# Adding a block's FFN rows to h in memory, and transforming the first filter block directly

## The chip, the cores and the metric

The kernel runs on one core of a Trainium2 chip. The metric is device time in microseconds of one execution, the median of the runs shown. The engines are TensorE (PE, with its weight loads PEld), VectorE (DVE), ScalarE (ACT), GpSimd (POOL) and SyncE (SP), which here only issues transfers.

## The reference

```python
k_shift = sum over t of k_pad[:, t:t + S, :] * shift_k[:, ks - 1 - t]   # ks = 4 taps
kv = k_shift * v
y  = irfft(rfft(kv, 2S) * rfft(ssm_k, 2S))[:S] + kv * ssm_D             # long causal convolution
h  = x + layernorm(x) * y                                               # x = q
h2 = h + (silu(layernorm(h) @ w_gate) * (layernorm(h) @ w_up)) @ w_down
```

S is 2048, D is 640, the FFN width is 1728, all in bf16. `h2` is the output.

## The kernel before

The sequence is cut into four blocks of 512 rows, each held as 128 partitions x 4 rows (`r`) x 640. For each block j the kernel makes a spectrum of kv and one of the filter block g, multiplies and accumulates the spectra of the earlier blocks with those of the filter, transforms back, forms h, and runs the FFN on it. FFN j-1 is written to run beside the convolution part of block j.

A spectrum is four real parts times two halves, held in a buffer `S` of 128 x 2 x 4 x 640. `transform` first makes the sums over the even rows (r = 0, 2) and the odd rows (r = 1, 3) by two products each (`sums_of`, L298), copies both out of PSUM (L303, by ACT or DVE), and then DVE makes odd minus and plus even (L318, L321). In block 0 this is done in two column halves of 320 (`SPLIT`). `mac` multiplies spectra on DVE (L442 for the first term, L464 and L465 for the others); `inverse` makes the back transform (DVE L529, L532, then products L540), normalises x (`applied`, L516), multiplies with the product in PSUM (L547) and adds to x (L550), so that x's buffer then holds h. `square_sums` (L475), `ln1` (L509) and `norm` give the two LayerNorms' statistics; ln1's `norm` runs on POOL. `turn_h` normalises h and transposes it to hT (L564, L566).

`ffn` makes gate and up products (L591) in seven weight groups, loaded by SP into two buffers `wgu`; ACT makes silu (L597) and copies the up part (L606), DVE multiplies them (L608) into tT. Then for each of four rows r it makes the down products (L641), two halves of 14 each, into one PSUM buffer. Ahead of the first of them stand two products of h with the identity (L637), which add h. ACT copies the row to `o` (L645), and SP stores it (L646). There is one `o` buffer, two PSUM buffers `ps_c` for the convolution and two `ps_f` for the FFN. Two buffers `x` hold q and then h; the next block's q can be loaded only when h is no longer read.

No operation is issued directly: each is added to a `Plan` with a duration, a priority, its buffers and dependences, and `schedule` picks again and again the operation that can start first by its estimates (`key = (at, prio, number)`). The result is a fixed order on each engine. An operation with an `other` way is placed on whichever of two engines can take it first. At run time each engine works through its list in order and waits for semaphores. So a change of one duration in the plan can move instructions on every engine.

Before the first block the queue of SP holds, in order, tapw and ident (small), k, v, the transform table WF, g, one row D, x, the back table WI and the first weights. DVE builds the diagonal tap matrices `diag` (L660) from ident and tapw; TensorE transposes k (L415) and convolves with `diag` (L429), and DVE multiplies by v (L432).

## Time and profile before

| | |
|---|---|
| runs | 309.61, 308.06, 307.67 us; median 308.06 |
| profiled execution | 308.97 us, its span 306.7 us |
| busy | PE 92%, DVE 75%, ACT 55%, POOL 11% of the span |
| mean granted TensorE clock | 0.967 |
| moved by DMA | 34.41 MB, mean 112 GB/s |

A busy TensorE is not TensorE at its peak, since products are pipelined and their ends modelled: in a row of a group, the mean duration of one product is its latency, and its pace is read from the chain, where the time of several is given. In a row of the chain stand the start, the time and the group with its count.

### The profile page before, as it was taken

The page shows a single profiled execution, that of the slowest core. Times are in us where ns is not written, and L with a number is a line of the kernel's source. Part 1 is how long each engine was busy: PE and PEld are TensorE (multiplying, and loading weights), DVE is VectorE, ACT ScalarE, POOL GpSimd, SP SyncE. Part 2 cuts the span into 40 slices and gives each one's busy share as a digit, 9 for nine tenths or more (in the row PEclk, how much of TensorE's full clock was granted, in tenths as well). Part 3 has the DMA queues.
Part 4 walks back from the last instruction along what each step waited for, and adds up shares of the span by engine and source line. Part 5 has one row for each costly group of instructions (what it writes and reads, how often), then busy time and mean ns, then how long its engine had stood idle before and what let it go on. Part 6 is the DMA issues. An engine that isn't in the chain of part 4 may idle for free.

```text
span 306.7 us, 4908 instructions
## 1 busy us (share of the span) xinstructions
PE 283.2 (92%) x1964; PEld 173.3 (56%) x1964; DVE 231.1 (75%) x316; ACT 168.6 (55%) x285; POOL 34.7 (11%) x52
## 2 busy tenths in 40 slices
PE   1994777799999999999999999999998999999995
PEld 1962445675555657665455578654444665444563
DVE  3599987988999999999979899999989840110200
ACT  2198967727875444548866770368743532445301
POOL 0000800810000000000270000001490000000000
PEclk9999795599999999999999999999999999999999
DMA  6999300114736250343651330316564001654011
GB/s 214 371 344 355 92 1 12 76 37 134 205 96 187 51 130 21 110 128 94 167 128 21 97 98 24 92 41 164 138 146 129 23 24 52 164 146 89 2 43 43
DMA packets 51512, 34.41 MB, mean 112 GB/s; under 512 B 12641, under 2 KB 49698, under 8 KB 51490
## 3 DMA queue, kind: packets, MB, share of 16 engines
q1 hardware_dynamic: 51490, 34.11, 38.5%
q8 instruction: 15, 0.25, 0.3%
q14 instruction: 7, 0.06, 0.1%
HBM read 31.48 MB, written 2.62 MB: 111 GB/s over the span
## 4 chain that ended last, share of the span: by engine, by line
PE 78%; DVE 12%; ACT 4%; POOL 2%; DMA 1%; issue 1%; SPq 0%; DVEq 0%; ACTq 0%; POOLq 0%
PE ps_f L591 32%; PE ps_f L641 20%; PE ps_c L298 8%; PE ps_c L429 6%; PE ps_c L540 4%; DVE S L442 2%; PE ps_f L637 2%; DMA ld<-in_A_k_dram 1%; PE ps_c L564 1%; ACT sg L606 1%; PE ps_c L415 1%; DVE row L547 1%; DVE S L321 1%; DVE S L318 1%; PE ps_f L429 1%
## 5 line engine op out<-in xcount | busy, mean ns | idle before, releaser
L591 PE MATMUL ps_f<-hT,wgu 128*128 128x512 bf16 x540 | 122.1, 379 | 0.0
L591 PEld LDWEIGHTS <-wgu 128*128 128x128 bf16 x540 | 52.3, 98 | 57.5 <-issue 0.3
L641 PE MATMUL ps_f<-wd,tT 128*128 128x320 bf16 x448 | 67.4, 299 | 0.0
L641 PEld LDWEIGHTS <-tT 128*128 128x128 bf16 x448 | 42.1, 98 | 19.4 <-issue 4.0
L597 ACT ACTIVATE sg<-ps_f 128x1024 bf16<-128x1024 f32 (+1 forms) x28 | 27.0, 963 | 31.5 <-PE ps_f L591 31.5
L608 DVE TENSOR_TENSOR tT<-sg,sg 128x1024 bf16<-128x1024 bf16 (+1 forms) x28 | 18.2, 650 | 33.1 <-ACT sg L606 32.9
L298 PE MATMUL ps_c<-t,WF 128*128 128x320 bf16 x224 | 39.8, 312 | 2.0 <-ACT scr L303 0.8
L465 DVE TENSOR_TENSOR S<-S,scr 128x2560 bf16<-128x2560 bf16 x24 | 35.8, 1492 | 0.8
L298 PEld LDWEIGHTS <-WF 128*128 128x128 bf16 x256 | 25.4, 101 | 18.5 <-issue 5.2
L464 DVE TENSOR_TENSOR scr<-S,S 128x2560 bf16<-128x2560 bf16 x24 | 35.6, 1484 | 0.0
L606 ACT CAST sg<-ps_f 128x1024 bf16<-128x1024 f32 (+1 forms) x28 | 26.6, 949 | 16.5 <-PE ps_f L591 15.2
L645 ACT CAST o<-ps_f 128x640 bf16<-128x640 f32 x16 | 11.1, 692 | 42.6 <-PE ps_f L641 41.6
L475 ACT ACTIVATE row<-x 128x640 bf16<-128x640 bf16 x32 | 23.5, 739 | 14.2 <-DVE x L550 13.7
L429 PEld LDWEIGHTS <-kT 128*128 128x128 bf16 x320 | 21.3, 107 | 1.8 <-DVE kT L417 0.7
L303 ACT CAST scr<-ps_c 128x640 bf16<-128x640 f32 (+1 forms) x30 | 19.2, 672 | 5.4 <-PE ps_c L298 5.2
L490 POOL TENSOR_TENSOR sm<-sm 128x4 f32<-128x4 f32 x4 | 3.1, 763 | 160.2 <-ACT row L509 160.2
L429 PE MATMUL ps_c<-diag,kT 128*128 128x128 bf16 x280 | 19.0, 231 | 0.2 <-ACT hT L566 0.2
L303 ACT CAST S<-ps_c 128x640 bf16<-128x640 f32 (+1 forms) x25 | 15.3, 643 | 4.9 <-PE ps_c L298 4.9
L540 PEld LDWEIGHTS <-WI 128*128 128x128 bf16 x128 | 12.6, 98 | 9.4 <-issue 3.8
L516 DVE TENSOR_SCALAR row<-x,sm 128x640 bf16<-128x640 bf16 x32 | 12.9, 442 | 1.4 <-POOL sm L502 1.2
L432 DVE TENSOR_TENSOR t<-ps_c,ld 128x640 bf16<-128x640 f32 x14 | 11.2, 819 | 2.4 <-PE ps_c L429 2.4
L547 DVE SCALAR_TENSOR_TENSOR row<-row,ps_c 128x640 bf16<-128x640 bf16 x14 | 11.5, 820 | 1.6 <-PE ps_c L540 0.5
(80 smaller groups left out, 291.2 us busy)
## 6 DMA issues: line engine op xcount, KB each, us to landing
wgu<-in_B_w_gate_dram SPq DMA_DIRECT2D x24, 320.0 KB, 3.1
wgu<-in_B_w_up_dram SPq DMA_DIRECT2D x24, 320.0 KB, 3.2
ld<-in_A_k_dram SPq DMA_DIRECT2D x4, 640.0 KB, 4.5
ld<-in_A_v_dram SPq DMA_DIRECT2D x4, 640.0 KB, 5.0
ld<-in_A_ssm_k_dram SPq DMA_DIRECT2D x4, 640.0 KB, 5.4
x<-in_A_q_dram SPq DMA_DIRECT2D x4, 640.0 KB, 6.0
out_dram<-o SPq DMA_DIRECT2D x16, 160.0 KB, 1.8
wd<-in_B_w_down_dram SPq DMA_DIRECT2D x1, 2080.0 KB, 12.0
```

Source lines behind the costliest of these rows:

```text
L298: nc.tensor.matmul(ap(ps)[:, w, 0:NH], ap(WF)[:, r, c, :], ap(src)[:, r, w * NH:(w + 1) * NH], start=(i == 0), stop=(i == 1))
L303: copy(two(cut(to(c)[2](), ws)) if len(ws) == 2 else cut(to(c)[2](), ws), half(ap(ps)) if len(ws) == 2 else ap(ps)[:, ws[0], 0:NH])
L429: nc.tensor.matmul(line(ap(ps))[:, c * P:(c + 1) * P], ap(kT)[:, c, q, off:off + P], ap(diag)[:, 4 * c + t, :], start=(t == 0), stop=(t == 3))
L464: nc.vector.tensor_mul(flat2(b), X.part(xs), H.part(hs))
L465: f(A.part(dst), A.part(dst), flat2(b))
L475: act(930, lambda r=r, junk=junk: nc.scalar.activation(ap(junk), ap(x)[:, r, :], ACT.Square, scale=D ** -0.5, accum_out=sm(s, 1)[:, r:r + ...
L540: nc.tensor.matmul(ap(ps)[:, w, 0:NH], ap(WI)[:, c, r, :], src[:, w * NH:(w + 1) * NH], start=(c == 0), stop=(c == 3))
L591: nc.tensor.matmul(ap(ps)[:, i, :], ap(w)[:, k, off:off + P], ap(hT)[:, k, :], start=(k == 0), stop=(k == KT - 1))
L597: act(580 * n + 20 if n == 1 else 1010, lambda: nc.scalar.activation(ap(sg)[:, 0:n, :], ap(gate[0])[:, gate[1]:gate[1] + n, :], ACT.Silu), ...
L606: nc.scalar.copy(ap(co)[:, 0:n, :], ap(up[0])[:, up[1]:up[1] + n, :])
L608: op.rest = dve(420 if n == 1 else 690, lambda: nc.vector.tensor_mul(ap(tT)[:, c:c + n, :], ap(sg)[:, 0:n, :], ap(co)[:, 0:n, :]), [sg, co ...
L641: nc.tensor.matmul(ap(ps)[:, hf, 0:NH], ap(tT)[:n, c, r * P:(r + 1) * P], ap(wd)[:n, c, hf * NH:(hf + 1) * NH], start=False, stop=(c == NC ...
```

## The change

Five things change together.

- In blocks 0 to 2 the identity products are gone. SP stores h of the whole block to the output (L634 in the new kernel) once h is complete; ACT copies the FFN row to `o` as before (L694), and a transfer issued by POOL adds it to the output in memory (L698). In block 3 DVE adds h while it reads the row from PSUM (L692), and SP stores it.
- The first g spectrum is made `straight`: each of its two halves by four products per part, with a table `minus` of negated weights for the odd rows, so that no add or subtract follows. The products per part are four in place of two. `minus` lies in the FFN's `tT` buffer, which is free then, and is one more load of 128 x 2048.
- The first loads: tapw and ident are issued by ACT; x comes right behind k, ahead of v; minus behind g.
- LN1 of block 0 has its `norm` on DVE in place of POOL. In blocks 2 and 3 kv's PSUM rows may be copied by ACT and multiplied on DVE from SBUF (`ACTKV`), and rows may be normalised by ACT (`ACTLN`), with the bias that `norm` now makes; `inverse` may place its row normalisations ahead of the products.
- The plan's estimates: a POOL transfer holds POOL's queue for 1300 ns and ends 1600 ns behind its data, POOL's norm takes 10000 for 4000, `applied` 450 for 260; down products wait in the plan for the last gate product.

The core of the diff:

```diff
-FLEX, LN1 = 100, 'pool'
+FLEX, DIRECT, ACTLN, ACTKV, ENDDVE = 100, ('G0',), 12, 12, True
...
+    ISSUE = {"sp": 450, "add": 1300}
+    QUEUE = {"add": "pool"}
...
-    def transform(src, dst, pieces):
-        for ws in pieces:
+    def transform(src, dst, pieces, minus=None):
+        for ws in pieces if minus else ():
+            for o in range(2):
+                for c in range(4):
+                    ps = conv_ps()
+                    def mm(o=o, c=c, ps=ps, ws=ws):
+                        for i, r in enumerate((0, 2, 1, 3)):
+                            m = ap(minus)[:, r // 2, c * P:(c + 1) * P] if o and r % 2 else ap(WF)[:, r, c, :]
+                            for w in ws:
+                                nc.tensor.matmul(ap(ps)[:, w, 0:NH], m, ap(src)[:, r, w * NH:(w + 1) * NH], start=(i == 0), stop=(i == 3))
+                    pe(545 * len(ws), mm, [src, WF, minus], [ps], [dst])
...
+        for ws in () if minus else pieces:
...
+            if plan.all >= ACTKV:
+                op = plan.add("act", 700, lambda r=r, ps=ps: nc.scalar.copy(ap(kv)[:, r, :], line(ap(ps))), [ps, v], [(kv, r)], (), ("dve", 820, straight))
+                op.rest = dve(490, lambda r=r: nc.vector.tensor_mul(ap(kv)[:, r, :], ap(kv)[:, r, :], rd(v)[:, r, :]), [v], [(kv, r)])
...
-        norm(s, nc.gpsimd if LN1 == 'pool' else nc.vector)
+        norm(s, nc.vector if plan.all < 2 else nc.gpsimd, bias=True)
...
+        if bias and plan.all >= ACTLN:
+            plan.add("act", 930, scalar, [(x, r), s], [row], holds, ("dve", 450, vector))
...
-    def ffn(j, hT, h):
+    def ffn(j, hT, h, end=False):
         tT = new("tT")
+        there = Buf(None)
+        if not end:
+            load(MB, lambda: nc.sync.dma_start(out=block(oo, j), in_=ap(h)), [there], [h])
...
-                    for hf in range(2):
-                        if lo == 0:
-                            nc.tensor.matmul(ap(ps)[:, hf, 0:NH], ap(ident), ap(h)[:, r, hf * NH:(hf + 1) * NH], start=True, stop=False)
...
-                pe(272 * (hi - lo + (lo == 0)), mm, [wd, (h, r), ident] + [(tT, c) for c in range(lo, hi)], [ps])
+                pe(272 * (hi - lo), mm, [wd] + [(tT, c) for c in range(lo, hi)], [ps])
+                plan.ops[-1].deps.add(behind)
             o = new("o")
-            act(700, lambda ps=ps, o=o: nc.scalar.copy(two(ap(o)), half(ap(ps))), [ps], [o])
-            load(MB / 4, lambda r=r, o=o: nc.sync.dma_start(out=block(oo, j)[:, r, :], in_=ap(o)), [], [o])
+            if end:
+                dve(820, lambda r=r, ps=ps, o=o: nc.vector.tensor_add(two(ap(o)), half(ap(ps)), two(ap(h)[:, r, :])), [ps, (h, r)], [o])
+            else:
+                act(700, lambda ps=ps, o=o: nc.scalar.copy(two(ap(o)), half(ap(ps))), [ps], [o])
+            if end:
+                load(MB / 4, lambda r=r, o=o: nc.sync.dma_start(out=block(oo, j)[:, r, :], in_=ap(o)), [], [o])
+            else:
+                plan.add("add", MB / 4 / 150.0, lambda r=r, o=o: nc.gpsimd.dma_start(out=block(oo, j)[:, r, :], in_=ap(o), accum_op=ALU.add), [o], [(there, r)])
...
-    G = [spectrum(gT, SPLIT)]
+    G = [spectrum(gT, SPLIT, minus if "G0" in DIRECT else None)]
...
-    ffn(*todo)
+    ffn(*todo, ENDDVE)
```

The order of the first loads on SP. Before:

```order
L650 DMA tapw<-in_A_shift_k_dram 128x5x4
L651 DMA ident<-const_ident 128x128
L272 DMA ld_77<-in_A_k_dram 128x2560
L272 DMA ld_78<-in_A_v_dram 128x2560
L654 DMA WF<-const_wf 128x2048
L265 DMA ld_79<-in_A_ssm_k_dram 128x5x512
L657 DMA row_87<-in_A_ssm_D_dram 1x640
L277 DMA x_75<-in_A_q_dram 128x2560
L659 DMA WI<-const_wi 128x2048
```

And now, where tapw and ident stand first on ACT:

```order
L275 DMA ld_77<-in_A_k_dram 128x2560
L280 DMA x_75<-in_A_q_dram 128x2560
L275 DMA ld_78<-in_A_v_dram 128x2560
L707 DMA WF<-const_wf 128x2048
L268 DMA ld_79<-in_A_ssm_k_dram 128x5x512
L711 DMA tT_84<-const_minus 128x2048
L713 DMA row_87<-in_A_ssm_D_dram 1x640
L714 DMA WI<-const_wi 128x2048
```

k is first in place of third, x second in place of eighth, and WI stays last of the tables, behind one more.

VectorE at the first g spectrum in block 0 (S0 is the spectrum of kv, S1 that of g, S2 their product). Before:

```order
L303 CAST S1_65<-ps_f0_97 128x320
L303 CAST scr2_74<-ps_c1_96 128x320
L318 TENSOR_TENSOR S1_65<-S1_65,scr2_74 128x4x320
L321 TENSOR_TENSOR S1_65<-S1_65,scr2_74 128x4x320
L442 TENSOR_TENSOR S2_66<-S0_64,S1_65 128x2x2x320
L442 TENSOR_TENSOR scr2_74<-S0_64,S1_65 128x4x320
L318 TENSOR_TENSOR S1_65<-S1_65,scr0_72 128x4x320
L321 TENSOR_TENSOR S1_65<-S1_65,scr0_72 128x4x320
L442 TENSOR_TENSOR scr1_73<-S0_64,S1_65 128x4x320
```

Now:

```order
L526 SCALAR_TENSOR_TENSOR sm0_99<-sm0_99 128x4
L510 SCALAR_TENSOR_TENSOR sm0_99<-sm0_99 128x4
L339 TENSOR_TENSOR S0_64<-S0_64,scr1_73 128x4x320
L342 TENSOR_TENSOR S0_64<-S0_64,scr1_73 128x4x320
L547 TENSOR_SCALAR row3_90<-x0_75,sm0_99 128x640
L547 TENSOR_SCALAR row1_88<-x0_75,sm0_99 128x640
L470 TENSOR_TENSOR S2_66<-S0_64,S1_65 128x2x2x320
L547 TENSOR_SCALAR row0_87<-x0_75,sm0_99 128x640
L470 TENSOR_TENSOR scr0_72<-S0_64,S1_65 128x4x320
```

The add and subtract on S1 are gone, and its evictions have all moved to ACT; the last of LN1's small operations and three row normalisations now stand between the kv spectrum and the first multiply.

ScalarE at the end of block 2's FFN (o is the row buffer, sm0 or sm3 block 3's statistics, hT block 3's). Before:

```order
L627 CAST sg0_92<-ps_f1_98 64x512
L475 ACTIVATE row0_87,sm3_102<-x1_76 128x640 x2
L475 ACTIVATE row1_88,sm3_102<-x1_76 128x640
L645 CAST o0_91<-ps_f0_97 128x640
L475 ACTIVATE row0_87,sm3_102<-x1_76 128x640
L645 CAST o0_91<-ps_f1_98 128x640
L566 COPY hT0_83<-ps_c1_96 128x5x128 x2
```

Now:

```order
L694 CAST o0_91<-ps_f0_97 128x640
L550 ACTIVATE row1_88<-x1_76,sm2_101 128x640
L550 ACTIVATE row2_89<-x1_76,sm2_101 128x640
L503 ACTIVATE row1_88,sm0_99<-x1_76 128x640
L694 CAST o0_91<-ps_f1_98 128x640
L503 ACTIVATE row1_88,sm0_99<-x1_76 128x640
L503 ACTIVATE row3_90,sm0_99<-x1_76 128x640
L503 ACTIVATE row1_88,sm0_99<-x1_76 128x640
L694 CAST o0_91<-ps_f0_97 128x640
L611 COPY hT0_83<-ps_c0_95 128x5x128 x2
L694 CAST o0_91<-ps_f1_98 128x640
```

The copies of o stand among block 3's sums, two of its row normalisations and its hT copies, and three of the four rows now go ahead of hT or between its copies, where two did. Each copy but the first waits for the transfer that adds the row before it.

108 lines of the change are left out of this document (67 added, 41 removed).

## The prediction

> **What bounds the kernel now.** I read the page's busy line, slices and chain first, then busy time by stretch, then the chain and the timeline around the stretches that differ.
>
> ```profile
> span 306.7 us, 4908 instructions
> PE 283.2 (92%) x1964; PEld 173.3 (56%) x1964; DVE 231.1 (75%) x316; ACT 168.6 (55%) x285; POOL 34.7 (11%) x52
> PE 78%; DVE 12%; ACT 4%; POOL 2%; DMA 1%; issue 1%; SPq 0%; DVEq 0%; ACTq 0%; POOLq 0%
> ...
> 20.00:30.00 10.00, 6.79 (x48) 4.05 (x47) 9.62 (x16) 9.09 (x26) 0.20 (x1) 1.00 1.03 378
> 30.00:40.00 10.00, 7.21 (x43) 4.43 (x43) 9.93 (x15) 9.59 (x21) 7.78 (x12) 0.83 0.24 74
> 50.00:60.00 10.00, 7.51 (x63) 6.19 (x62) 9.45 (x21) 9.00 (x16) 5.35 (x6) 0.50 0.20 66
> ...
> 100.00:120.00 20.00, 19.92 (x169) 13.02 (x167) 19.14 (x33) 9.80 (x16) 0.00 (x0) 1.00 0.29 77
> 120.00:140.00 20.00, 20.00 (x165) 13.40 (x163) 19.08 (x16) 9.76 (x16) 0.00 (x0) 1.00 0.31 93
> ```
>
> The columns after the stretch are PE, PEld, DVE, ACT, POOL, granted clock, DMA share and GB/s. Two regimes show. From 20 to 40 us VectorE is full (9.62 and 9.93 of 10) while TensorE has three idle microseconds in ten. From about 60 us on TensorE is full (20.00 of 20), with VectorE close behind at 95%. So a TensorE product costs little in the first regime and its whole pace in the second; a VectorE operation is the other way round. The profiled execution took 308.97 us, span 306.7 plus 2.27 around it; the median of the runs shown is 308.06, that is 0.9 below. My sum is made on 308.97.
>
> **Identity products.** Thirty-two products (x with ident) go, eight per block.
>
> ```profile
> L637 PE MATMUL ps_f<-x,ident 128*128 128x320 bf16 x32 | 7.0, 301 | 1.6 <-ACT sg L606 1.3
> ...
> 115.87 1.36 PE ps_f L641 x10
> 286.47 3.91 PE ps_f L641 x28
> 290.75 3.91 PE ps_f L641 x28
> ```
>
> The mean of 301 ns is latency; the pace is 1.36 us for ten products of that shape, 0.136 each, so 32 x 0.136 = 4.4 us. All lie behind 109 us, where TensorE is full, so all of it is on the path. The upper end is the joint in the last block: 286.47 + 3.91 = 290.38 to 290.75 is 0.37 per pair, 16 x 0.37 = 5.9 us, if the whole joint goes. I take 4.4, since changing rows should keep some of the joint. In the new order ten transposes of g(2), 0.056 each (0.56 for ten, below), stand behind block 0's last hT transpose instead of ahead of it: +0.6. What is left for TensorE from there on falls by 3.8 us.
>
> ```profile
> 76.61 0.56 PE ps_c L333 x10
> 62.47 1.08 PE ps_f L591 x5
> ```
>
> **First g spectrum made straight.** It adds 32 products (64 for 32), 4.4 us of TensorE, and takes four half-width VectorE add/subtracts away, all before 38 us.
>
> ```profile
> 25.31 0.83 DVE L318 TENSOR_TENSOR S<-S,scr 128x1280 bf16<-128x1280 bf16 x1
> ...
> 27.03 0.83 DVE L442 TENSOR_TENSOR S<-S,S 128x1280 bf16<-128x1280 bf16 x1
> 36.00 1.55 DVE L442 TENSOR_TENSOR S<-S,scr 128x1280 bf16<-128x1280 bf16 x2
> 37.47 0.81 DVE L529 TENSOR_TENSOR scr<-S 128x1280 bf16<-128x1280 bf16 x1
> ...
> 38.33 0.70 PE L540 MATMUL ps_f<-scr,WI 128*128 128x320 bf16 x4 [1.05 <-DVE scr L529]
> 41.62 0.82 DVE L547 SCALAR_TENSOR_TENSOR row<-row,ps_f 128x640 bf16<-128x640 bf16 x1 [0.52 <-PE ps_c L540]
> ```
>
> VectorE up to the first inverse product (38.33): four add/subtracts, 25.31 to 27.03 being 1.72 per pair, about -3.3; the order has five half-width evictions on it for twelve, 7 x 0.48 = -3.4; one more gT copy, priced like such an eviction, +0.5; the first LN1's ten small operations, which POOL did before, at their pace of about 0.2 (the LN2 twin below: 51.40 to 53.43) +2.0; three row normalisations moved ahead, 3 x 0.44 = +1.3. Sum -2.9.
>
> ```profile
> L303 DVE CAST scr<-ps_c 128x320 bf16<-128x320 f32 x5 | 2.3, 483 | 0.1
> L516 DVE TENSOR_SCALAR row<-x,sm 128x640 bf16<-128x640 bf16 x32 | 12.9, 442 | 1.4 <-POOL sm L502 1.2
> 51.40 0.16 DVE L482 SCALAR_TENSOR_TENSOR sm<-sm,sm 128x4 f32<-128x4 f32 x1
> 53.43 1.71 DVE L516 TENSOR_SCALAR row<-x,sm 128x640 bf16<-128x640 bf16 x4
> ```
>
> **First loads.** tapw and ident go to ACT's queue, so k is issued first on SP instead of third:
>
> ```profile
> 0.72 0.44 SPq L650 DMA_DIRECT2D tapw<-in_A_shift_k_dram  x1
> 1.77 0.42 SPq L272 DMA_DIRECT2D ld<-in_A_k_dram  x1
> 6.26 0.71 PE L415 MATMUL ps_f<-ident,ld 128*128 128x128 bf16 x5 [6.26 <-DMA ld<-in_A_k_dram]
> 9.17 2.07 PE L429 MATMUL ps_f<-diag,kT 128*128 128x128 bf16 x19 [0.48 <-DVE kT L417]
> 13.47 1.13 PE ps_c L429 x20
> 15.50 0.44 PE ps_c L333 x5
> ```
>
> Issue 1.05 us earlier; TensorE waited 6.26 us for it, and diag (ready at about 7) begins to bind, so I take 0.9. Moved past in SP's queue: x goes before v, and the minus table (0.5 MB, 1.4 us at 378 GB/s) before WI and the weights; v is needed only at about 10, the products that use WI start past 34. With the DVE sum: 38.3 - 2.9 - 0.9 = 34.5.
>
> TensorE must agree. The convolution ends at 14.6 - 0.9 = 13.7; then 0.3 for the last kv row, 32 x 0.136 = 4.4, four g transposes 1.3 (14.6 to 15.94), 64 x 0.136 = 8.7: 28.4. An eviction (0.4 and 0.3 of hand-over), six multiply-adds at 0.74 (two in 1.47, from the rows at 36.00 and 37.47) and one subtraction at 0.8: 34.4. The later of the two is 34.5, with the hand-over 34.6: **-3.7 us**. TensorE is now the co-bound, so less VectorE work there would bring nothing more. Without the earlier k it is -2.8.
>
> **From the inverse to hT.** Three row normalisations are already made, -1.3; three full evictions on VectorE for a kT copy and an add, about +0.5: -0.8. Against it stands the clock. TensorE idled from 28.2 to 31.0 and then ran at half speed:
>
> ```profile
> 28.00:30.00 2.00, 0.17 (x4) 0.07 (x2) 1.97 (x3) 2.00 (x7) 0.00 (x0) 1.00 0.93 384
> 32.00:33.00 1.00, 1.00 (x7) 0.55 (x5) 1.00 (x2) 0.85 (x3) 0.92 (x2) 0.50 0.00 0
> 35.00:36.00 1.00, 0.97 (x7) 0.47 (x5) 1.00 (x3) 1.00 (x4) 0.92 (x2) 1.00 0.67 237
> ```
>
> Before, that slow stretch lay under VectorE's work. Now, from 28.4 on, TensorE has about 2.2 us of transposes and two g(1) groups and then waits for the multiply-adds until 34.6, so the slow stretch falls on the inverse. Its 24 first-and-second-half products took 38.33 to 41.6, 3.3 us; the first half of them at half clock costs +1.6, all of them +3.3. I take 1.6. The Trainium skill (TensorE: Matmul & The Clock Gate, section "Part 1: The HAM clock gate") says that an idle window of about 3.4 us halves the clock until a busy one has passed. The trace agrees: 0.50 at 32 to 33 and 1.00 from 35. Early part together: -3.7 - 0.8 + 1.6 = -2.9.
>
> **Adding transfers.** Each row of o in blocks 0 to 2 is now added to memory by a POOL-issued transfer, and there is one o buffer: ACT's next row copy waits until the transfer has landed, and behind it on ACT are evictions, LayerNorm sums and, in block 2, the copies of block 3's hT. The trace has no such transfer. Its neighbours:
>
> ```profile
> L645 ACT CAST o<-ps_f 128x640 bf16<-128x640 f32 x16 | 11.1, 692 | 42.6 <-PE ps_f L641 41.6 <-ACT scr L303 1.0
> DMA to landing us min/median/max: 1.8/1.8/3.9
> 225.96 0.20 POOL L495 TENSOR_TENSOR sm<-sm 128x4 f32<-128x4 f32 x1
> 228.47 1.45 POOL L502 TENSOR_TENSOR sm<-sm 128x4 f32<-128x4 f32 x1
> L501 POOL TENSOR_SCALAR sm<-sm 128x4 f32<-128x4 f32 x8 | 6.4, 800 | 0.7
> ```
>
> (The second row is for the plain stores of o.) Copy to copy, a plain store costs 0.69 + 1.8 = 2.5 us: the lower end. Upper end: two POOL steps each held behind a VectorE operation, 2 x 1.45, and the slowest landing, 3.9: 0.69 + 2.9 + 3.9 = 7.5. I take 0.69 + 0.8 (a POOL operation) + 1.8 + another 1.8, since memory must be read before it is written: 5.1, an estimate. The products between row ends in the new order, at 0.136, 0.056 and 0.216, give row spacings of 5.5, 6.0, 4.9 us in block 0, 4.4, 3.8, 7.1 in block 1, 1.1, 8.2, 3.8 in block 2. At 5.1 blocks 0 and 1 absorb it (15.3 against 16.4 and 15.3); in block 2 the copies run 1 to 2 late, and hT behind them half a microsecond: +0.5. By the Trainium skill (DMA: Bandwidth & Descriptors, "Anatomy of one DMA — SWDGE (gpsimd) path"), with about 2.0 us fixed and bytes / 436 GB/s, the cycle would be an estimated 0.69 + 1 + 2.4 = 4.1, and the term zero.
>
> The three 640 KB stores of h stand in SP's queue ahead of k(2) and between the next block's weight loads, and wait for VectorE's last write of h. I cost them at nothing: when the weights behind them come due, two loaded weight groups, 2 x 20 x 0.216 = 8.6 us of products, are still ahead; without that cover a store would cost as long as h is late. The end: the last row leaves by a VectorE add (0.82, as the PSUM read at 41.62) for ACT's 0.69: +0.1. Moving kv evictions and row normalisations of blocks 2 and 3 to ACT (9.8 of 20 busy) frees VectorE of 8 x (0.82 - 0.49) + 6 x 0.44 = 5.3 us; under a full TensorE I count it as nothing.
>
> **Sum:** -3.8 - 2.9 + 0.5 + 0.1 = -6.1. 308.97 - 6.1 = 302.9 profiled, and 0.9 less for the median: **302.0 us**.
>
> **Rivals.**
>
> *The adding transfers pace the down stages (slower).* Place: ACT's wait for the one o buffer. If POOL's work for a transfer is held behind VectorE's operations as its small ones are (0.20 free, 1.45 beside them) the cycle nears 7.5. Three cycles per block are 22.5 us against spacings of 16.4, 15.3 and 13.1, and the second PSUM buffer spares one row, 3.8, 3.8 and (two gate groups) 3.3: lost 2.3 + 3.4 + 6.1 = 11.8 us, that is 313. It turns into over 1% slower when 9 cycles pass 44.8 + 10.9 + 9.2, at 7.2 us, and at 6.0 if the spare row is worth nothing. For it: VectorE is 95% busy there. Against: POOL has nothing else to do in those stages. The Trainium skill (SBUF — State Buffer, "Who interferes with whom") has VectorE's two-input operations keep GpSimd from reading, not from writing the transfer's descriptors; only its copy and scalar forms would. By that rule the rival is mostly off; no run here shows it yet. Chance 0.16.
>
> *VectorE becomes the bound.* TensorE's 3.8 us return as waits for the multiply-adds: 305.8. For it: 19.1 of 20 busy. Against: before, TensorE reached block 3's gates at 256.71, some 5 us after hT was made (below), and VectorE sheds 5.3. Chance 0.12.
>
> ```profile
> 251.27 0.49 DVE L566 COPY hT<-ps_c 128x640 bf16<-128x640 bf16 x1 [1.43 <-PE ps_c L564]
> 256.71 28.18 PE ps_f L591 x130
> ```
>
> *The clock eats the early gain.* All of the inverse, and what follows to hT, runs at half clock: the -2.9 goes, 304.9. For it: 0.50 in the whole of 50 to 60. Chance 0.10.
>
> **How the numbers follow.** The forecast case has 0.62. One per cent, 3.1 us, is about what a measurement of this kernel can tell from none; faster means below 305.0, slower above 311.1. The forecast case lies at 298 to 305 by its bounds (identity joints 5.9, clock 0: -1.5 and -1.6, -0.5 for the adds, gives 298.4; clock 3.3 and no earlier k gives 304.6): faster 0.60, same 0.02. Adds: 0.04, 0.06, 0.06. VectorE: 0.03, 0.07, 0.02. Clock: 0.06, 0.04, 0. Together 0.73, 0.19, 0.08. The range 298.4 to 308.0 leaves out the worst of the adds and little below.
>
> **What would show it.** Right: the first inverse product at about 34.6, hT of block 0 about 3 us earlier, no identity line, row to row in the last block 3.9 to 4.0 us; adds whose o copies wait under 1 us each on ACT. Wrong: ACT's o copy with long waits on the transfer; the clock at 0.50 through the inverse; TensorE idle before block 3's gates; or k's products no earlier than 6.2 us.

## The result and the profile after

The changed kernel takes 301.36 us, the median of four runs (300.51 to 301.68), against 308.72 for the kernel before, measured with it (four runs, 307.67 to 309.61). The ratio is 0.976, with a 95% interval of 0.9736 to 0.9784. The forecast was 302.0. The profiled execution took 300.51 us: a span of 298.7 and 1.81 around it. It is the only one of the four with a mean granted clock of 1.000; the others have 0.993 to 0.994 and took 0.6 to 1.2 us longer.

The total came out close, but the places did not. First the page of the changed kernel: the span, the busy line and the granted clock by slice.

```profile
span 298.7 us, 4920 instructions
PE 276.9 (93%) x1964; PEld 170.0 (57%) x1964; DVE 227.2 (76%) x315; ACT 176.8 (59%) x299; POOL 27.2 (9%) x58
PEclk9999999999999999999999999999999999999999
```

TensorE is 6.3 us less busy, and the granted clock shows no slow slice (a 9 stands for 90% and more; the mean is 1.000). The next rows are the windows of the changed kernel, with the columns as in the prediction (PE, PEld, DVE, ACT, POOL, granted clock, DMA share, GB/s).

```profile
30.00:40.00 10.00, 7.15 (x60) 5.02 (x59) 9.87 (x15) 9.14 (x20) 0.00 (x0) 1.00 0.27 88
50.00:60.00 10.00, 7.46 (x94) 5.64 (x92) 9.52 (x21) 8.43 (x17) 2.65 (x4) 1.00 0.45 161
```

TensorE is no busier than it was before (7.15 against 7.21 of 10 between 30 and 40 us, 7.46 against 7.51 between 50 and 60), but between 50 and 60 us it runs at 1.00 where it ran at 0.50. Now the start of the changed kernel, as the timeline shows it: the issues of the taps, k and the identity, the two instructions that wait for the identity, and the last two groups of the convolution.

```profile
0.72 0.47 ACTq L702 DMA_DIRECT2D tapw<-in_A_shift_k_dram  x1
0.72 0.38 SPq L275 DMA_DIRECT2D ld<-in_A_k_dram  x1
1.22 0.54 ACTq L703 DMA_DIRECT2D ident<-const_ident  x1
...
7.79 0.69 PE L436 MATMUL ps_f<-ident,ld 128*128 128x128 bf16 x5 [7.79 <-DMA ident<-const_ident]
7.84 2.82 DVE L715 TENSOR_TENSOR diag<-ident,tapw 128x2560 bf16<-128x2560 bf16 x1 [6.90 <-DMA ident<-const_ident]
...
15.27 2.07 PE L450 MATMUL ps_f<-diag,kT 128*128 128x128 bf16 x20
17.18 1.28 PE L450 MATMUL ps_c<-diag,kT 128*128 128x128 bf16 x20
```

The identity is issued at 1.22 us, as it was before, but lands 6.5 us later instead of 2.8. The kernel before began its diagonal product at 4.15 us and its first transposes at 6.26. The convolution ends at 18.46 us (17.18 and 1.28), where it ended at 14.59. Its products also ran slowly for longer: ten of them took 1.07 us until about 16.9 us and 0.56 after that; in the kernel before the step came at about 11.0. The granted clock is given as 1.00 there all the same. Here are two rows of the timeline of the kernel before that the prediction did not show: the diagonal product, and the first convolution product of block 1 behind block 0's hT.

```profile
4.15 2.82 DVE L660 TENSOR_TENSOR diag<-ident,tapw 128x2560 bf16<-128x2560 bf16 x1 [3.21 <-DMA ident<-const_ident]
...
58.21 4.26 PE L429 MATMUL ps_c<-diag,kT 128*128 128x128 bf16 x40 [0.19 <-ACT hT L566]
```

The same marks in the changed kernel's timeline: the first inverse product, the first convolution product of block 1, the last of block 3's hT transposes, its gates, and the last two row additions.

```profile
39.42 0.70 PE L582 MATMUL ps_f<-scr,WI 128*128 128x320 bf16 x4 [2.12 <-DVE scr L567]
56.33 1.28 PE L450 MATMUL ps_c<-diag,kT 128*128 128x128 bf16 x20 [0.16 <-ACT hT L611]
248.21 0.72 PE L609 MATMUL ps_c<-ident,row 128*128 128x128 bf16 x10 [0.50 <-ACT hT L611]
249.60 29.30 PE L639 MATMUL ps_f<-hT,wgu 128*128 128x512 bf16 x135 [0.67 <-DVE hT L611]
291.12 0.82 DVE L692 TENSOR_TENSOR o<-ps_f,x 128x640 bf16<-128x640 f32 x1 [3.19 <-PE ps_f L686]
295.13 0.82 DVE L692 TENSOR_TENSOR o<-ps_f,x 128x640 bf16<-128x640 f32 x1 [3.19 <-PE ps_f L686]
```

With these marks the two profiled executions can be compared stretch by stretch (us; the marks of before are 14.59, 38.33, 58.21 and 256.71):

| stretch | before | after | difference | by the prediction's terms |
|---|---|---|---|---|
| start to the convolution's end | 14.59 | 18.46 | +3.9 | -0.9 |
| to the first inverse product | 23.74 | 20.96 | -2.8 | -2.8 |
| to block 1's first convolution product | 19.88 | 16.91 | -3.0 | +0.8 (-0.8 + 1.6) |
| to block 3's gates | 198.5 | 193.27 | -5.2 | -2.2 (24 products -3.3, transposes +0.6, adds +0.5) |
| to the end of the span | 49.99 | 49.1 | -0.9 | -1.0 (8 products -1.1, tail +0.1) |
| around the span | 2.27 | 1.81 | -0.5 | 0 |
| sum | 308.97 | 300.51 | -8.5 | -6.1 |

The stretch from the convolution to the inverse and the last block went as forecast. The start was 4.8 us worse than forecast, and the two stretches between inverse and block 3's gates were 3.8 and 3.0 better. These are single executions: the run with plain transfers below, which has the same start, has its first inverse product 1.15 us earlier, at 38.27.

The adding transfers, from the changed kernel's waits and DMA issues:

```profile
ACT o L694 <- DMA out_dram<-o: 1.7, 1, 1.7
out_dram<-o POOLq DMA_DIRECT2D x12, 160.0 KB, 3.4
DMA to landing us min/median/max: 3.3/3.4/5.8
```

POOL takes 0.88 us on average for an issue, the transfer lands 3.4 us after it began (the median), and ACT's copies waited for a landing once, 1.7 us.

### The profile page after: what moved, and what is told of

It is laid out like the page before. It is cut to its first block, busy times and chain, and to the rows that moved or that the text cites. A ratio compares the mean times of both kernels' runs of the same rounds, so it can differ in the third digit from the quotient of the medians.

```text
span 298.7 us, 4920 instructions
## 1 busy us (share of the span) xinstructions
PE 276.9 (93%) x1964; PEld 170.0 (57%) x1964; DVE 227.2 (76%) x315; ACT 176.8 (59%) x299; POOL 27.2 (9%) x58
## 4 chain that ended last, share of the span: by engine, by line
PE 85%; DVE 8%; ACT 3%; DMA 2%; issue 1%; ACTq 0%; DVEq 0%
PE ps_f L639 38%; PE ps_f L686 21%; PE ps_c L301 8%; PE ps_c L450 6%; PE ps_c L582 4%; DMA ident<-const_ident 2%; PE ps_f L325 1%; PE ps_c L325 1%; PE ps_f L450 1%; PE ps_c L609 1%; ACT hT L611 1%; DVE row L592 1%; DVE S L470 1%; DVE diag L715 1%; PE ps_c L354 1%; PE ps_c L436 1%
## 5 line engine op out<-in xcount | busy, mean ns | idle before, releaser
L686 PE MATMUL ps_f<-wd,tT 128*128 128x320 bf16 x448 | 66.3, 300 | 0.2
L654 ACT CAST sg<-ps_f 128x1024 bf16<-128x1024 f32 (+1 forms) x27 | 25.5, 946 | 17.5 <-PE ps_f L639 17.4
L301 PE MATMUL ps_c<-t,WF 128*128 128x320 bf16 x208 | 33.9, 299 | 2.0 <-DVE row L592 1.3
L301 PEld LDWEIGHTS <-WF 128*128 128x128 bf16 x224 | 21.5, 98 | 14.1 <-issue 3.7
L503 ACT ACTIVATE row<-x 128x640 bf16<-128x640 bf16 x32 | 23.5, 740 | 8.0 <-DVE x L595 7.4
L698 POOL DMA_DIRECT2D out_dram<-o x12 | 10.6, 883 | 154.5 <-ACT o L694 154.5
L306 ACT CAST scr<-ps_c 128x640 bf16<-128x640 f32 (+1 forms) x28 | 17.9, 672 | 5.0 <-PE ps_c L301 5.0
L306 ACT CAST S<-ps_c 128x640 bf16<-128x640 f32 (+1 forms) x22 | 13.7, 660 | 10.2 <-PE ps_c L301 10.2
L611 ACT COPY hT<-ps_c 128x640 bf16<-128x640 bf16 x12 | 8.1, 695 | 9.5 <-PE ps_c L609 9.5
L694 ACT CAST o<-ps_f 128x640 bf16<-128x640 f32 x12 | 8.3, 693 | 8.9 <-PE ps_f L686 7.2
L539 ACT ACTIVATE row<-x 128x640 bf16<-128x640 bf16 x16 | 11.8, 740 | 1.2 <-DMA x<-in_A_q_dram 1.2
```

Of the source, the lines that this page charges most:

```text
L301: nc.tensor.matmul(ap(ps)[:, w, 0:NH], ap(WF)[:, r, c, :], ap(src)[:, r, w * NH:(w + 1) * NH], start=(i == 0), stop=(i == 1))
L306: copy(two(cut(to(c)[2](), ws)) if len(ws) == 2 else cut(to(c)[2](), ws), half(ap(ps)) if len(ws) == 2 else ap(ps)[:, ws[0], 0:NH])
L503: act(930, lambda r=r, junk=junk: nc.scalar.activation(ap(junk), ap(x)[:, r, :], ACT.Square, scale=D ** -0.5, accum_out=sm(s, 1)[:, r:r + ...
L654: nc.scalar.copy(ap(co)[:, 0:n, :], ap(up[0])[:, up[1]:up[1] + n, :])
L686: nc.tensor.matmul(ap(ps)[:, hf, 0:NH], ap(tT)[:n, c, r * P:(r + 1) * P], ap(wd)[:n, c, hf * NH:(hf + 1) * NH], start=(c == 0), stop=(c == ...
```

## The experiments

The kernel before, measured again beside these runs, had medians of 308.17 to 308.43 us, against 308.72 beside the changed kernel. Differences of a few tenths between runs below are not told apart.

**The identity on SP's queue again.** My theory was that the identity's late landing cost the changed kernel its early gain.

```diff
-    plan.add("aq", 1900, lambda: nc.scalar.dma_start(out=ap(tapw), in_=...), [], [tapw])
-    plan.add("aq", 1900, lambda: nc.scalar.dma_start(out=ap(ident), in_=id_h.ap()), [], [ident])
+    def small():
+        nc.sync.dma_start(out=ap(tapw), in_=...)
+        nc.sync.dma_start(out=ap(ident), in_=id_h.ap())
+    plan.add("aq", 1900, small, [], [tapw])
+    plan.add("aq", 1900, None, [], [ident])
```

> The changed kernel with one thing undone: the taps and the identity are loaded again by the first two transfers on SP's queue, ahead of k, and not from ACT's queue; the order on every other engine is that of the changed kernel. Theory A (the identity's late landing cost the changed kernel its early gain): the diagonal product starts near 4.2 us instead of 7.84, the first transposes near 6.3 instead of 7.84, the convolution near 9.2 instead of 11.13 and ends near 14.6 instead of 18.5, the first inverse product stands 3 to 4 us earlier than 39.42 (near 36), and the time is 297.5 to 298.5 us. Rival B (the early stretch is set by VectorE or by the landing of v, g and the matrices, and the identity is hidden): the diagonal is earlier, but the first inverse product stays within 1 us of 39.4 and the time within 300.5 to 302. Rival C (an earlier convolution only lengthens TensorE's idle time ahead of the inverse, and the granted clock falls again as in the kernel before): first inverse product near 36, granted clock 0.50 for some 10 us after it, time 300 to 302.

Measured: 298.34 us (six runs, 296.72 to 300.43), ratio to before 0.9669 (0.9637 to 0.9701). From the timeline of this kernel:

```profile
3.40 2.83 DVE L718 TENSOR_TENSOR diag<-ident,tapw 128x2560 bf16<-128x2560 bf16 x1 [2.46 <-DMA ident<-const_ident]
...
35.87 1.22 PE L582 MATMUL ps_f<-scr,WI 128*128 128x320 bf16 x4 [2.13 <-DVE scr L567]
36.88 1.27 PE L582 MATMUL ps_c<-scr,WI 128*128 128x320 bf16 x4
37.95 1.25 PE L582 MATMUL ps_f<-S,WI 128*128 128x320 bf16 x4
...
54.34 1.28 PE L450 MATMUL ps_c<-diag,kT 128*128 128x128 bf16 x20 [0.16 <-ACT hT L611]
```

The first inverse product stands 3.55 us earlier, and the time is 3.0 us less. Theory A holds, and rival B falls. Rival C holds in part: groups of four products, which start 0.54 us apart in the changed kernel, start 1.07 apart here (36.88 and 37.95), and the stretch to block 1's convolution takes 18.47 us instead of 16.91. Of 3.55 us, 1.55 are lost there again. Not all of the 3.55 is the identity, either: the convolution ends at 14.90 here, at 18.46 in the changed kernel and at 17.30 in the run with plain transfers, where the identity is as late (its diagonal starts at 7.80) but the products' pace rose earlier. Against that run, whose inverse also began at half clock, the small loads on SP's queue give 2.4 us at the inverse and 2.5 us of the span (299.2 and 296.7).

**Which place makes a small transfer late?** First the two transfers on ACT's queue swapped:

```diff
+    plan.add("aq", 1900, lambda: nc.scalar.dma_start(out=ap(ident), in_=id_h.ap()), [], [ident])
     plan.add("aq", 1900, lambda: nc.scalar.dma_start(out=ap(tapw), in_=...), [], [tapw])
-    plan.add("aq", 1900, lambda: nc.scalar.dma_start(out=ap(ident), in_=id_h.ap()), [], [ident])
```

> The changed kernel with the two transfers on ACT's queue swapped: the identity first, then the taps. Theory A (both share the transfer engines with k, q, v and WF, which SP issues at the same time, and so land late whatever their turn): the identity lands at 6.5 to 7.7 us again, the first transposes start near 7 to 7.8, the time stays within 1 us of 301.4. Rival B (the identity was late because it stood behind the taps' 640 small pieces in its own queue): it lands before 5 us, the first transposes start at 6.2, when k has landed, and the diagonal product still waits for the taps.

Measured: 304.0 us (two runs), 2.6 slower than the changed kernel. From its timeline:

```profile
0.73 0.37 ACTq L702 DMA_DIRECT2D ident<-const_ident  x1
1.13 0.53 ACTq L703 DMA_DIRECT2D tapw<-in_A_shift_k_dram  x1
4.94 0.71 PE L436 MATMUL ps_f<-ident,ld 128*128 128x128 bf16 x5 [4.94 <-DMA ld<-in_A_k_dram]
10.41 2.83 DVE L715 TENSOR_TENSOR diag<-ident,tapw 128x2560 bf16<-128x2560 bf16 x1 [9.47 <-DMA tapw<-in_A_shift_k_dram]
```

Now the identity is in time and the transposes wait for k alone, at 4.94; but the taps, 5 KB, are late, by more than the identity was. Theory A falls. Rival B is right in what it says of the identity, but it named the taps' pieces as the reason, and the second transfer on that queue is late whichever of the two it is.

Next a queue for each, with fillers that the run after next explains:

```diff
-    plan.add("aq", 1900, lambda: nc.scalar.dma_start(out=ap(tapw), in_=...), [], [tapw])
+    plan.add("aq", 1900, lambda: nc.gpsimd.dma_start(out=ap(tapw), in_=...), [], [tapw])
```

> The changed kernel with the identity alone on ACT's queue, the taps alone on POOL's queue, k first on SP's queue, and the 12 unread products of 128x192 in TensorE's idle time ahead of the first inverse product. Theory A (a small transfer that is the first of its queue lands before the large ones of the other queues, and only a second one is late): identity and taps have both landed when k has, near 4.9 us, the diagonal product starts near 4 us, the convolution near 8 us, the first inverse product near 34.5, and the time is 295.7 to 296.7 us, faster than every kernel so far. Rival B (only a place ahead of k in k's own queue lands early): the taps land near 8 to 10 us, the convolution starts at 11 to 14 us, and the time is 301 to 304 us.

Measured: 300.82 us (300.35 to 301.14). The timeline of this kernel, and its DMA issues in the last two rows:

```profile
1.28 1.07 POOL L708 DMA_DIRECT2D tapw<-in_A_shift_k_dram  x1 [0.85 <-POOLq L791]
7.96 2.83 DVE L721 TENSOR_TENSOR diag<-ident,tapw 128x2560 bf16<-128x2560 bf16 x1 [7.01 <-DMA tapw<-in_A_shift_k_dram]
...
ident<-const_ident ACTq DMA_DIRECT2D x1, 32.0 KB, 3.6
tapw<-in_A_shift_k_dram POOLq DMA_DIRECT2D x1, 5.0 KB, 6.6
```

The taps are the first and only transfer of POOL's queue, and still late: theory A falls as I put it. Rival B's numbers are nearly met (7.9, 10.8 and 300.82 us), but not its reason, since the identity on ACT's queue is in time. What the late ones have in common is the time of issue: 1.13, 1.22 and 1.28 us, half a microsecond after k's 640 KB were issued at 0.73. Those issued with k or ahead of it were in time. That the time of issue is the cause is an inference: no run issues a small transfer late and alone on ACT's queue, and POOL's queue may be slow with 640 pieces for reasons of its own. So the taps went first on SP's queue, ahead of k, and the identity alone on ACT's, issued at the same moment:

```diff
-    plan.add("aq", 1900, lambda: nc.scalar.dma_start(out=ap(tapw), in_=...), [], [tapw])
+    plan.add("aq", 1900, lambda: nc.sync.dma_start(out=ap(tapw), in_=...), [], [tapw])
```

> As the kernel with three queues, but with the taps first on SP's queue, ahead of k, and the identity alone on ACT's. Theory A: the taps land near 3 us, k 0.45 us later than when it is first, the first transposes start near 5.3, the convolution near 8.3, the time is 296 to 297 us. Rival B (the identity is late on ACT's queue whether alone or not): first transposes near 7.5 us, time 299 to 301 us.

Measured: 296.71 us (four runs, 296.01 to 297.58), ratio to before 0.9621 (0.9586 to 0.9656). Its timeline:

```profile
0.73 0.39 ACTq L709 DMA_DIRECT2D ident<-const_ident  x1
0.73 0.44 SPq L708 DMA_DIRECT2D tapw<-in_A_shift_k_dram  x1
1.23 0.51 SPq L275 DMA_DIRECT2D ld<-in_A_k_dram  x1
3.14 2.83 DVE L721 TENSOR_TENSOR diag<-ident,tapw 128x2560 bf16<-128x2560 bf16 x1 [2.19 <-DMA tapw<-in_A_shift_k_dram]
5.27 0.72 PE L442 MATMUL ps_f<-ident,ld 128*128 128x128 bf16 x5 [5.27 <-DMA ld<-in_A_k_dram]
...
34.76 0.70 PE L588 MATMUL ps_f<-scr,WI 128*128 128x320 bf16 x4 [1.14 <-DVE scr L573]
51.68 1.28 PE L456 MATMUL ps_c<-diag,kT 128*128 128x128 bf16 x20 [0.16 <-ACT hT L617]
```

This is the fastest kernel of the study, 4.65 us below the changed kernel. Theory A's numbers hold (5.3, 8.2, 296 to 297). For the identity the queue is not what decides: on ACT's queue it was late when issued behind k and in time when issued with k or ahead of it. For the taps, queue and order of issue changed together in every run where their landing shows, so they are not separated.

**The clock ahead of the inverse.** In the kernel with the small loads on SP's queue, 12 products that nothing reads were put into the idle 2.13 us ahead of the first inverse product. They write PSUM columns 320 to 511, which the spectra leave free, so that no engine's order changes. (The kernel that was fastest and the one with three queues have them too.)

```diff
+    made, FILL = [0], {18: 12}
...
+                    made[0] += 1
+                    for i in range(FILL.get(made[0], 0)):
+                        nc.tensor.matmul(ap(ps)[:, 0, NH:512], ap(WF)[:, 0, 0, :], ..., start=True, stop=True)
```

> The kernel with the small loads on SP's queue, and in TensorE's idle time of 2.13 us ahead of the first inverse product 12 products of 128x192 more, whose results go to columns that nothing reads; every engine's order is otherwise the same. Theory A (that idle time is what lets the granted clock fall to 0.50 just as the inverse starts): the clock stays at 1.00 from 30 to 45 us in every run, the first three inverse groups take 0.54 us each instead of 1.07 to 1.22, the stretch from the first inverse product to block 1's first convolution product after the hT transposes takes 16.9 us instead of 18.5, and the median is 296 to 297.2 us with a narrower spread. Rival B (the clock falls for another reason, for instance the work done before it): the clock falls as it did, and the time stays at 297.7 to 299. Rival C (the added products come in the way of the inverse): first inverse product later than 36.3, time 298.3 to 299.5.

Measured: 297.39 us (297.0 to 297.63). Its timeline:

```profile
35.65 0.70 PE L588 MATMUL ps_f<-scr,WI 128*128 128x320 bf16 x4 [1.14 <-DVE scr L573]
...
52.57 1.28 PE L456 MATMUL ps_c<-diag,kT 128*128 128x128 bf16 x20 [0.16 <-ACT hT L617]
```

The stretch from the inverse takes 16.92 us, as forecast, 1.55 less than without the products, and the granted clock is 0.997 to 1.000 in all five runs (0.989 to 0.999 without). The median fell by 0.95, a little less than theory A had it, and the runs lie closer together. With 1.14 us of idle time left in place of 2.13 the clock stays up.

The same in the kernel before, in its two longest idle times:

```diff
+    made, FILL = [0], {38: 12}
...
+                for i in range(9 if turns[0] == 6 else 0):
+                    nc.tensor.matmul(ap(pt)[:, 1, 0:NH], ap(WF)[:, 0, 0, :], ..., start=True, stop=True)
```

> The kernel before, with unread products in two idle times of TensorE: 9 of 128x320 in the 2.8 us from 28.1 us, and 12 of 128x192 in the 2.05 us from 42.3 us; every engine's order is otherwise the same, and nothing of the change is in it. Theory A (the half clock from 45.5 to 62.3 us costs the kernel before some 5 us, and that, not VectorE, is most of what the straight spectrum gave): the clock stays at 1.00 through most of 30 to 62 us and the time is 303 to 304.5 us. Rival B (VectorE sets the pace there and the half clock is hidden beside it): the clock is 1.00 and the time within 1 us of 308.4. Rival C (idle time is not what lowers the clock): the clock is 0.50 as before, the time 308 to 309.5.

Measured: 307.59 us (12 runs, 306.77 to 309.28), ratio 0.9978 (0.9956 to 1.0000). Windows of this kernel:

```profile
40.00:50.00 10.00, 7.61 (x66) 5.51 (x64) 8.95 (x20) 6.64 (x15) 0.64 (x1) 1.00 0.00 1
50.00:60.00 10.00, 6.39 (x62) 5.25 (x59) 9.46 (x20) 8.50 (x16) 5.89 (x9) 0.66 0.21 67
```

Theory A's time is not met, but the run is no full test of it. The clock came back between 40 and 50 us (0.75 before), but it was still near half from 32 to 36 us, behind 1.8 us of idle time that the first filler left, and it fell again at 53 us, in an idle time of 1.1 us. The stretch from the first inverse product to block 1's convolution shrank from 19.88 to 18.77 us, and that convolution's first 40 products from 4.26 to 3.31, while the first inverse product came 0.7 us later (39.04). The median fell by 0.6. What a whole clock would be worth in the order of the kernel before stays open. Its runs alone suggest that a half clock is cheap there: those with a mean clock of 0.967 took 308.8 to 309.6 us, those with 0.983 took 307.6 to 308.4; 0.016 of 307 us are 10 us at half clock, for some 1.2 us.

**Without the straight g spectrum.**

```diff
-FLEX, DIRECT, ACTLN, ACTKV, ENDDVE = 100, ('G0',), 12, 12, True
+FLEX, DIRECT, ACTLN, ACTKV, ENDDVE = 100, (), 12, 12, True
```

> The changed kernel without the straight g spectrum: block 0's g spectrum is made by sums and differences again (8 products of two terms for each half with VectorE's subtractions and additions), and the negated matrices are not loaded; the planner orders the rest anew. Theory A (the straight spectrum fills TensorE ahead of the inverse, and that keeps the granted clock at 1.00): the clock falls to 0.50 around 32 to 62 us as in the kernel before, the stretch from the first inverse product to block 1's first convolution product takes near 19.9 us instead of 16.9, the first inverse product is no earlier than 39.4, and the time is 305 to 308 us. Rival B (the clock stayed up only because the whole start moved later by the identity's late landing): the clock stays at 1.00 and the time is 301 to 304, the loss being VectorE's 3.3 us of sums at most. Rival C (the straight spectrum buys nothing, since TensorE pays for it what VectorE saves): 300.5 to 302.

Measured: 304.79 us (304.62 to 305.05), 3.4 more than the changed kernel. Its timeline:

```profile
41.62 1.23 PE L582 MATMUL ps_f<-scr,WI 128*128 128x320 bf16 x4 [4.54 <-DVE scr L567]
61.50 1.28 PE L450 MATMUL ps_c<-diag,kT 128*128 128x128 bf16 x20 [0.78 <-ACT hT L611]
```

TensorE idles 4.54 us, and the inverse begins at half clock, as theory A said. From the convolution's end to the first inverse product it takes 24.09 us (17.53 to 41.62), against 20.96 with the straight spectrum. The next stretch takes 19.88 us; that this is the figure of the kernel before is chance, since here the mark is the second convolution group of block 1, and a first one stands ahead of hT (56.12). The time is 0.2 below theory A's range. But A does not yet say how much is clock and how much VectorE. So the same kernel with 40 unread products in the 4.54 us:

```diff
+    made, FILL = [0], {38: 40}
```

> The changed kernel without the straight g spectrum, with 40 unread products of 128x192 in TensorE's idle time of 4.54 us ahead of the first inverse product, which hold the clock where the straight spectrum held it. Theory A (of the 3.4 us that the straight spectrum is worth, about half is the clock and half VectorE's relief): the inverse runs at 0.54 us for a group of four, its first product stands at 41 to 42 us, and the time is 302.5 to 303.8 us. Rival B (the clock is hidden beside VectorE there, and all 3.4 us are VectorE's): 304.3 to 305. Rival C (it is all the clock): 301.2 to 302.

Measured: 302.23 us (301.71 to 302.65). Its timeline:

```profile
41.14 0.70 PE L588 MATMUL ps_f<-scr,WI 128*128 128x320 bf16 x4 [1.24 <-DVE scr L573]
...
58.55 1.28 PE L456 MATMUL ps_c<-diag,kT 128*128 128x128 bf16 x20 [0.78 <-ACT hT L617]
```

Products that compute nothing recover 2.6 of the 3.4 us (304.79 to 302.23); the order is otherwise the same, and the stretch behind the inverse's start shrinks from 19.88 to 17.41 us. That does not leave only 0.9 for VectorE, since this kernel is filled and the changed kernel is not: filling brought 0.95 us in the other start (298.34 to 297.39). A filled partner would take an estimated 301.36 - 0.95 = 300.4 us; the kernel with three queues, filled and with a late start, took 300.82. Against these the straight spectrum still saves 1.4 to 1.8 us with the clock held up on both sides. VectorE's relief is whole at the first inverse product, where both kernels without the straight spectrum need 24.09 us from the convolution's end and the kernels with it 20.97. So about half of the 3.4 us is the clock and half VectorE's work, as theory A had it, though the time lies 0.3 below its range. The clock here was at 0.83 between 50 and 60 us, so the division is rough.

**The FFN.** The identity products back in the changed kernel, in blocks 0 to 2:

```diff
-            load(MB, lambda: nc.sync.dma_start(out=block(oo, j), in_=ap(h)), [there], [h])
...
+                    if lo == 0 and not end:
+                        for hf in range(2):
+                            nc.tensor.matmul(ap(ps)[:, hf, 0:NH], ap(ident), ap(h)[:, r, hf * NH:(hf + 1) * NH], start=True, stop=False)
...
-                plan.add("add", ..., nc.gpsimd.dma_start(out=block(oo, j)[:, r, :], in_=ap(o), accum_op=ALU.add), [o], [(there, r)])
+            load(MB / 4, lambda r=r, o=o: nc.sync.dma_start(out=block(oo, j)[:, r, :], in_=ap(o)), [], [o])
```

> The changed kernel with the identity products put back in the FFN of blocks 0 to 2 (24 products of 128x320 more, two for each of 12 rows), rows stored plainly from SP's queue, and no store of h and no adding transfers; the rest as in the changed kernel (the last block still adds h on VectorE). Theory A (TensorE is saturated there and each pair costs its issue time of 0.27 us): 12 x 0.27 = 3.3 us more, 304.3 to 305.2 us, granted clock 1.00 throughout. Rival B (the adding transfers cost nearly what the products cost): 301 to 303. Rival C (the gain of the FFN came from more than the products, for instance from the order of the planner): over 305.5.

Measured: 303.96 us (303.37 to 304.75), 2.6 more than the changed kernel and between A and B. In its profile the clock was down at the inverse (0.80 between 40 and 45 us) and at one more place, block 1's first convolution product:

```profile
56.93 2.27 PE L450 MATMUL ps_c<-diag,kT 128*128 128x128 bf16 x20
```

From there to the end of the span it took 245.8 us, the changed kernel 242.4; about 1.0 of the 3.4 is this group at half clock, so 2.4 are left for products that take 3.3. TensorE's waits for hT ahead of block 3's gates, 1.17 us in the changed kernel, are not there; one of 0.59 for ACT's sg is. The other side, the changed FFN alone in the kernel before (the changed `ffn` with its store of h, adding transfers and last additions, and nothing else):

> The kernel before with the changed FFN alone: h of blocks 0 to 2 stored whole, rows added to it by transfers from POOL's queue, the last block's h added on VectorE, no identity products; the loads, the spectra, the inverse and the norms as before. Theory A (32 products of 0.136 us, 4.35 us of a TensorE without idle time, less some 0.5 us): 304 to 305 us. Rival B (a part of the products' time comes back as idle time, since the down products were also filler): 305.3 to 306.5. Rival C (the FFN carries nearly the whole change): under 303.

Measured: 304.16 us (303.20 to 305.07), ratio 0.985 (0.9812 to 0.9889), 4.15 below the kernel before measured beside it (308.31): theory A. Its timeline:

```profile
57.77 4.39 PE L431 MATMUL ps_c<-diag,kT 128*128 128x128 bf16 x40 [0.18 <-ACT hT L568]
252.60 0.72 PE L566 MATMUL ps_c<-ident,row 128*128 128x128 bf16 x10 [0.50 <-ACT hT L568]
254.09 29.30 PE L596 MATMUL ps_f<-hT,wgu 128*128 128x512 bf16 x132 [0.77 <-DVE hT L568]
```

From 57.77 to 254.09 it takes 196.3 us, 2.2 less than before (198.5), though 3.3 us of products went. TensorE waited for hT 2.2 us in all, 0.93 at 120.44 and 0.50 and 0.77 ahead of block 3's gates; the kernel before had none of these, but waited 1.35 us for ACT's sg ahead of block 2's first identity product. So 0.85 us came back as idle time. The changed kernel has the waits ahead of block 3's gates too (0.50 and 0.67), and not the other.

**Plain transfers in place of adding ones.**

```diff
-... nc.gpsimd.dma_start(out=block(oo, j)[:, r, :], in_=ap(o), accum_op=ALU.add), [o], [(there, r)])
+... nc.gpsimd.dma_start(out=block(oo, j)[:, r, :], in_=ap(o)), [o], [(there, r)])
```

> The changed kernel with the 12 transfers of FFN rows on POOL's queue writing plainly instead of adding; this leaves out the sum with h in blocks 0 to 2, so those rows of the output lack it. Theory A (the adding transfers are hidden but for the 1.7 us in all by which ACT's copies wait on them, off the path): landing falls from 3.4 us to near 2.5, and the time stays within 0.5 us of the changed kernel's, 300.9 to 301.7. Rival B (reading back while adding slows the down stages): 299.5 to 300.5 or less. Rival C (the issue on POOL is the price, not the adding): landing and time unchanged.

Measured: 300.75 us (300.44 to 301.02), 0.6 below the changed kernel, between theories A and B. Its DMA issues, and two rows of its timeline:

```profile
out_dram<-o POOLq DMA_DIRECT2D x12, 160.0 KB, 2.1
...
38.27 1.10 PE L582 MATMUL ps_f<-scr,WI 128*128 128x320 bf16 x4 [2.13 <-DVE scr L567]
...
56.86 1.28 PE L450 MATMUL ps_c<-diag,kT 128*128 128x128 bf16 x20 [0.17 <-ACT hT L611]
```

Adding costs 1.3 us of landing. But from 56.86 to the end of the span, 299.2, it is 242.3 us, against 242.4 in the changed kernel: in the stretch where the adding transfers are, they cost no more than 0.1, and the 0.6 between the medians is not theirs.

**The inverse made straight too**, in the kernel with the small loads on SP's queue:

```diff
-FLEX, DIRECT, ACTLN, ACTKV, ENDDVE = 100, ('G0',), 12, 12, True
+FLEX, DIRECT, ACTLN, ACTKV, ENDDVE = 100, ('G0', 'inv0'), 12, 12, True
```

> The kernel with the small loads on SP's queue, with block 0's inverse made straight too: 8 terms per product and no differences and sums on VectorE ahead of it. It takes 4 operations of 0.74 to 0.82 us off VectorE and gives TensorE 32 products of 128x320 more, 0.136 us each by the groups of four at 0.54: 4.3 us. Theory A (VectorE sets the pace from the spectra to the hT transposes, and TensorE has idle time there): the first inverse product stands 0.7 us earlier, the time is 296 to 297.8 us. Rival B (TensorE's added 4.3 us land on the path between the inverse and hT): 299 to 302.

Measured: 298.21 us (297.01 to 299.02), the same as without (298.34) within what can be told. Its timeline:

```profile
28.88 0.43 PE L582 MATMUL ps_f<-S,WI 128*128 128x320 bf16 x2
47.31 1.24 PE L639 MATMUL ps_f<-hT,wgu 128*128 128x512 bf16 x5
```

The first inverse product stands 7.0 us earlier, where theory A had 0.7. The first gate product stands at 47.3 us, against 55.45 without, but TensorE has 4.3 us more to do, and it waits 2.9 us in all at block 2's down products (for sg) and ahead of block 3's gates (for a normalised row and hT), where it waits 1.2 without. Block 1's transposes of k and its convolution, which stood ahead of the first gate product, now in part stand behind it. Neither theory's mechanism tells the whole: the first gate came 8 us earlier, and the end hardly moved.

## Why the prediction was nearly right, and where it was wrong

The number, 302.0 for 301.36, stands on errors that cancel: the start 4.8 us too good, the stretches from the inverse to block 3's gates 6.8 too bad, the time around the span 0.5 too long. The profiled execution came out at 300.51 where the sum had 302.9. The sum then put the median 0.9 below the profiled execution, as it had been before, and it lies 0.85 above. That the medians meet is luck.

*The identity products (-4.4, with the transposes -3.8): right.* The FFN alone gave -4.15. The second rival, VectorE as the bound, did not come in: waits of 1.17 us for hT appeared ahead of block 3's gates, but the 1.35 us for ACT's sg ahead of block 2's identity products went, and TensorE's idle time between the marks fell from 1.60 to 1.33 us. Of the ten transposes five still stand ahead of the mark, so they cost 0.3 in place of 0.6. The joint in the last block is as forecast, or 0.01 above it: row to row 4.01 us (291.12 to 295.13).

*VectorE up to the first inverse product (-2.9): right.* From the convolution's end it took 23.74 us before and 20.96 now, and 20.97 in every other run with the straight g spectrum and the inverse as it is.

*"First loads" (k 0.9 us earlier): the step that failed.* It followed k, and k did land earlier, at 4.50 us. It did not follow the two transfers that moved to make room. The forecast had the convolution end at 13.7 us; it ended at 18.46. With the identity 6.5 us under way, its run of products began 2.9 us later than forecast (11.13 for 8.27), and then took 1.9 us longer than before, at half pace until about 16.9 us (before, until 11.0). The run with the small loads on SP's queue prices the late loads at 3.0 us of the time (2.5 against the run with plain transfers). Where taps, identity and k all land early, the first inverse product stands at 34.76; the forecast was 34.6.

*The clock (+1.6): the right size where it happens, but not in the profiled execution.* In four profiles with the same idle time ahead of the inverse the clock fell there, and the stretch took 18.05 to 18.78 us in place of 16.92. The changed kernel's profiled execution lost nothing there; its other three runs, with clocks of 0.993 to 0.994 and 0.6 to 1.2 us more, may well have, but where their clock fell is not on record. What the sum left out was the other side. It said that the slow stretch of the kernel before at 32 to 35 us "lay under VectorE's work", and gave no term to the second one, 0.50 from 46 to 62 us. Behind hT that one was on the path: block 1's first 40 convolution products took 4.26 us, and 2.4 where the clock is whole; that alone is about 2 of the 3.0 us that the stretch to block 3's gates did better. Filling idle time in the changed order without the straight spectrum brought 2.6 us; in the order of before it brought 0.6, with part of the half clock left. In the stretch before it, from the inverse to block 1's convolution, the clock can be most of the 3.0 us: filling alone took 2.5 off it in the changed order without the straight spectrum (19.88 to 17.41). So the straight spectrum gave two things where I had counted one, less work for VectorE and a TensorE that stays busy, and of its 3.4 us about half is each.

*The adding transfers (+0.5, cycle 5.1 us): over-priced.* The cycle is 0.69 + 3.4 = 4.1 us, and they cost no more than 0.1 in their stretch. The estimate that the prediction gave from the Trainium skill's figures (DMA: Bandwidth & Descriptors, "Anatomy of one DMA — SWDGE (gpsimd) path") was 4.1 too, which is partly luck: it has no part for the adding, and a plain transfer, for which it would be the same, landed in 2.1 us and not in 3.4. The first rival, with a cycle past 6 us, falls: POOL's issues took 0.86 us (median) with VectorE full beside them, and 0.86 in the one at 250.27 us with VectorE idle, so they were not held. The rule of the Trainium skill (SBUF — State Buffer, "Who interferes with whom") that weighed against this rival agrees with that.

*Stores of h, the end, VectorE's later relief at nothing:* nothing in the trace contradicts them; no run tries them alone. *The clock eats the early gain*, the third rival, did not happen at its place; the loads, and the slow products of the convolution, ate it.

By single runs the 7.4 us are: the FFN -4.15, the straight spectrum -3.4 (about half of it by the clock), the late small loads +3.0. That leaves -2.8, by subtraction and only if the parts add up, for what no run tried alone: q loaded ahead of v, the first LN1 on VectorE, the evictions and normalisations moved to ACT, and the planner's order. Also open is the 0.46 us around the span; the FFN alone has it too (305.07 for a span of 303.3).

## What to carry to other kernels

When loads change places, follow every one that moves to the instruction that waits for it, the small ones first: here 32 KB issued half a microsecond after 640 KB cost about 3 us. Price a step by everything that its region runs out of: the straight spectrum gave VectorE less to do and TensorE something to do without a break, about half its gain each, and a few unread products in TensorE's idle time tell the two apart. Fill both kernels that you compare, or neither. A sum that comes out right is no proof of its terms; marks along the timeline, stretch by stretch, are, as far as one profiled execution stands for the rest.
